# First Gram by whole 64x64 blocks, and a new order of the copies, roundings and second solver in the head of a fused attention and MLP kernel

## The chip, the cores and the metric

The kernel runs on one core of a Trainium2 chip. The metric is the time of one execution in microseconds, as the device measures it; three runs were made of the kernel before. One further execution was profiled. The engines are TensorE (PE in the profile, with its weight loads as PEld), VectorE (DVE), ScalarE (ACT), GpSimd (POOL) and SyncE (SP, which issues most DMAs).

## What is computed

Three stages follow one another. The first is a chunked delta-rule attention, the second an MLP with a gate that mixes along the sequence, the third another MLP; here they are in the reference, cut down:

```python
k_n = k / (norm(k, axis=-1) + 1e-06)            # batch 4, heads 8, seq 768, dim 48
for t in range(S):
    y[t] = q[t] @ state
    state = state + beta[t] * outer(k_n[t], v[t] - k_n[t] @ state)
x = y as (4, 768, 384)
h = gelu(x @ w_in)                               # 384 -> 1024, tanh form
u, v = h[..., :512], h[..., 512:]
gated = u * (w_sg @ layernorm(v, g_ln) + b_sg)   # w_sg mixes the 768 positions
x = x + gated @ w_out
xk, xr = mu_k * x + (1 - mu_k) * x_prev, mu_r * x + (1 - mu_r) * x_prev
out = sigmoid(xr @ w_r) * (relu(xk @ w_k) ** 2 @ w_v)
```

## The kernel before, in words

**Attention.** The 768 steps are cut into 12 chunks `s` of 64 steps, two chunks making one of NG = 6 groups `g`. The 32 pairs of batch and head lie as 16 columns on two halves of the partitions, and in two halves `o` of 8 columns each. For a group, `gram(g)` forms k k^T: for each of four blocks `i` PE makes 64 small products (32x32 and 64x32, L331 and L333) into a PSUM bank, then ACT copies the diagonal 32x32 blocks into GD and the off-diagonal ones into GL (both L340). `solver(g)` on DVE transposes GD (L358), normalizes, and inverts the unit triangular 32x32 blocks by products and sums (L353, L391); its last instruction is the transposition into DT (L438). `couple(g, k)` then multiplies GL with DT on PE (L452) and copies back on ACT (L455); a chunk's stage `st_n` needs it (`joined`).

For each chunk and half run five stages: `st_rq` (state times k and q on PE, L493 and L496; a copy r32 on ACT for group 0, L468, else an addition on DVE, L470; two copies of Q on ACT, L508, and masks on POOL, L509), `st_d` (DT times r32, L516; copy u1 on ACT, L521), `st_n` (L529, copies L535), `st_s` (the state's update, L544, copies L550) and `st_y` (L558, copy yst L563, then the stores to xT by SP). `scale_v` on POOL (L460) scales the values by the norms that solver(0) gave. A fixed list `slots` sets the order of the stages, one slot after another; `run` issues a slot, calls `tick` three times and then `fill`.

**Projections.** When both chunks of a group have their y, `x_split` makes the high part of x on ACT (L118) and the low part on POOL (L121); `push` then puts the units of that group on a list: `v_units` (PE L628, ACT L637 with the gelu, then a layernorm stream) and `u_units` (PE L680). `fill(n)` issues n products' worth of them; a v unit is ready when 6 and a u unit when 12 of the roundings of w_in are done. Where units run out, `keep_warm` issues products over a tile of zeros instead (L719), into a bank that nothing reads.

**Roundings.** The weights are split into a high and a low part that PE multiplies in three terms. One split is a job `narrow`: a DMA into `raw`, a conversion on ACT (L162), four steps on DVE (L167, L169, L171, L173), an addition on POOL (L175), the high half on ACT (L118), the low half on POOL (L121). There are three buffers `raw` and two `na`. The twelve jobs of w_in (six for the v columns, named wiv, six for the u columns, wiu) come first, then those of w_out and w_k.

**What sets the order.** PE, ACT, DVE and POOL are scheduled by hand: each engine does its instructions in the order in which the program issues them. `background(t)` gives out t units of time among three kinds of streams (ln, solve, jobs) in proportion to SHARE, with `spent` the account; an action put off by `after(n, f)` is done n points later. `point` counts the ticks. Ahead of the stages a prologue issues the first two Grams, the whole of solver(0), and what is in the list `rest`, one entry a step.

The lines that set the second solver and the first couples in order:

```python
        keep_warm(JS)
        point[0] = 0
        for e in streams:
            e[0] = 0
        later += [(3 + k, lambda k=k: couple(0, k)) for k in range(2)]
        ...
            if n == 0 and g + 1 < NG:
                streams.append([point[0] + SOLVE0, solver(g + 1), "solve"])
            background(BUDGET * (B0 if g == 0 else 1))
```

The functions that the change touches, whole:

Of the kernel before, what the change touches and what calls it, by code (L numbers as in the profile page):

```python
# [7 lines left out]
F32 = mybir.dt.float32  # L8
# [12 lines left out]
P = 128  # L21
C = 64
# [12 lines left out]
SV = 60  # L35
B0 = 1.0
PRE = 0.8
GRAM0 = 17
SOLVE0 = 1
# [9 lines left out]
LAGC = 2  # L49
JS = 18  # L50
NT_ = (3, 3, 3)
LNW = 1
LAGX = 6
LAGE = (4, 1)
LASTP = 134
FROM = 125
LAGU = 5
COST = dict(rq=1.05, d=0.8, n=0.8, s=0.85, y=1.1)
SHARE = ((1, 12, 1), (1, 4, 1), (2, 8, 2))
NRAW = 3  # L60
# [24 lines left out]
def fused_kernel(  # L85
# [142 lines left out]
    def slot(tag, shape, dtype=F32):  # L228
        return wq.tile(shape, dtype, name="s" + tag, tag=tag)
# [13 lines left out]
    with ExitStack() as at:  # L243
# [41 lines left out]
        def bank():  # L285
# [9 lines left out]
               ap1.tile([P, NU, 32], F32, name="GL")]  # L295
        DTb = [slot(W0[3], [P, NU, 32]), ap1.tile([P, NU, 32], F32, name="DT")]
        V.memset(Dm, 0.0)
        unit = ap1.tile([P, P], F32, name="unit")
# [19 lines left out]
        def gram(g, parts=((0, 64),)):  # L318
# [3 lines left out]
            def half(i, c0, c1, j):  # L322
# [13 lines left out]
                if j:  # L336
# [6 lines left out]
            return [[(0, lambda i=i, j=j, c=c: half(i, *c, j)) for j in range(2)]  # L343
                    for c in parts for i in range(4)]

        Yt = ap1.tile([P, 16, 16], F32, name="Yt")
# [9 lines left out]
        def solver(g):  # L356
# [62 lines left out]
            for last in (0, 1):  # L419
# [9 lines left out]
                for i, (ov, args) in enumerate(ops):  # L429
                    tv, t = product(*args)  # L430
                    yield t
                    if g == 0 and last and i == 1:
                        V.memset(warm, 0.0)
                    if g == 0 and last and i == 2:
                        scale_v(0)
                    yield total(ov, tv, t)
# [115 lines left out]
        def st_y(s, o):  # L552
# [13 lines left out]
            if s % 2:  # L566
                store_x(g, o, ysts[o])
                after(LAGX if g < NG - 1 else LAGE[o], lambda: splits.append((g, o)))
            if o == 1:
# [25 lines left out]
        def x_split(g, o):  # L595
# [8 lines left out]
            split(A, G if g < NG - 1 else V, xs, xh, xl)  # L604
            after(LAGU, lambda: push(g, o, xh, xl))
            return True
# [85 lines left out]
        def fill(n):  # L692
# [14 lines left out]
            if n > 0 and point[0] < 144:  # L707
                idle[0] += min(n, WARM) if point[0] <= 36 else n
                keep_warm(int(idle[0]))
                idle[0] -= int(idle[0])  # L710
# [66 lines left out]

        early(1, 0.01)
        for o in range(2):
            load_q(0, o)  # L780
        load_tok(0)
        diag = gram(0, ((0, 32), (32, 64)))
        for job in diag[:4]:
            for _, f in job:
                f()
            early(1, NPRE)
        streams.append([point[0], solver(0), "solve"])
# [3 lines left out]
        def whole(job):  # L791
            for _, f in job:
# [3 lines left out]
                 ((st_n, 0, 0), (st_rq, 1, 0)), ((st_d, 1, 0), (st_s, 0, 0), (st_y, 0, 0))]  # L796
        rest = [lambda j=j: whole(j) for j in diag[4:]]
        k = 0
        while any(e[2] == "solve" for e in streams):
            early(1, PRE)  # L800
            k += 1
            if k == 2:
# [4 lines left out]
                nc.sync.dma_start(out=mu_sb, in_=mu)  # L807
            if 0 in neTs and 1 not in GDs:
                after(SV, lambda: scale_v(1))
                body = st_rq(0, 0)  # L810
                rest.append(lambda: next(body))
                rest += [lambda j=j: whole(j) for j in gram(1)]
            if rest:
                rest.pop(0)()
        for f in rest:
            f()
        next(body, None)
        next(body, None)
        keep_warm(JS)
# [4 lines left out]
        later[:] = [(i, f) for i, (_, f) in enumerate(later)]  # L824
        later += [(3 + k, lambda k=k: couple(0, k)) for k in range(2)]
        used[0] = 0

        def tick():
# [3 lines left out]
            if nn == 0 and 0 <= gg and gg + 2 < NG:  # L832
                grams.extend(gram(gg + 2))
            if n == 0 and g + 1 < NG:
                streams.append([point[0] + SOLVE0, solver(g + 1), "solve"])
# [362 lines left out]
```

## Time and profile before

| | us |
|---|---|
| median of three runs | 776.47 (773.41 to 778.66) |
| the profiled execution | 771.39 |
| its span | 769.7 |
| PE busy | 697.1 (91%) |
| DVE busy | 507.0 (66%) |
| ACT busy | 372.9 (48%) |
| POOL busy | 200.6 (26%) |

The mean granted clock of PE in that execution is 0.968 of full. Shares of busy time are means over the three stages of the program; the head, in which the first two solvers run, is a little over an eighth of the span. The chain that ended last has 70% on PE and 12% on DVE. In a row of the timeline stand the start in us from the start of the span, the duration, the engine, the line, the operation, what it writes and reads with the names of the program's tiles, shapes, the count, and in brackets how long the engine idled before and what released it. Names are those of the storage: `sg`, `ms`, `rk`, `qk` and so on are buffers that several tiles share.

### The profile page before, as it was taken

To read this page: it belongs to the slowest core of one execution; us is meant where nothing else is said; L and a number is where in the kernel's file an instruction comes from. 1 tells how busy PE (TensorE), PEld (TensorE's weight loads), DVE (VectorE), ACT (ScalarE), POOL (GpSimd) and SP (SyncE) were. 2 spreads that over 40 slices of the span, in tenths; PEclk is the share of its full clock that TensorE was granted. 3 is DMA by queue.
4 is the path that set the end of the run, shared out by engine and by line. 5 is a ranking of instruction groups with operands and counts; after the bars stand their busy time and mean duration, and the time that the engine had idled before them with its cause. 6 is when DMAs were issued, how large, how long until landed. Compare 5 with 4: busy or idle time off the path is not lost.

```text
span 769.7 us, 24933 instructions
## 1 busy us (share of the span) xinstructions
PE 697.1 (91%) x10820; PEld 648.8 (84%) x10820; DVE 507.0 (66%) x1071; ACT 372.9 (48%) x752; POOL 200.6 (26%) x246
## 2 busy tenths in 40 slices
PE   3559799898998998888889979999999999999998
PEld 3437688787887886687889979999999999999997
DVE  6989999697797884532286867289564564563441
ACT  3236576766765767653332322147454453462330
POOL 3034635353454554430235341210000000000000
PEclk9978899999999999999989999999999999999999
DMA  8413445565565566556467562327000000000000
GB/s 238 93 41 100 131 123 153 129 185 163 148 185 155 159 171 181 194 149 198 143 229 244 178 195 79 110 87 194 22 11 32 21 11 32 21 10 32 11 22 32
DMA packets 82159, 88.76 MB, mean 115 GB/s; under 512 B 24704, under 2 KB 65024, under 8 KB 82048
## 3 DMA queue, kind: packets, MB, share of 16 engines
q1 hardware_dynamic: 76816, 77.92, 34.2%
q0 software_dynamic: 4800, 9.04, 4.3%
q8 instruction: 85, 1.39, 0.7%
q14 instruction: 26, 0.21, 0.1%
q10 hardware_dynamic: 432, 0.20, 0.1%
HBM read 56.60 MB, written 25.82 MB: 107 GB/s over the span
## 4 chain that ended last, share of the span: by engine, by line
PE 70%; DVE 12%; DMA 5%; issue 4%; POOL 3%; ACT 2%; SPq 1%; POOLq 0%; DVEq 0%; ACTq 0%
PE ms L149 36%; PE ms L944 7%; PE ms L628 6%; PE ms L680 5%; PE ms L558 3%; DVE sg L353 3%; PE rk L516 2%; PE sps L544 2%; PE rk L529 2%; PE rk L493 2%; PE ms L452 2%; POOL na L175 2%; DVE sg L391 1%; PE ms L331 1%; DVE Yt L391 1%
## 5 line engine op out<-in xcount | busy, mean ns | idle before, releaser
L149 PE MATMUL ms<-wvh,sl 128*128 128x384 f32 x192 | 64.6, 336 | 0.0
L149 PE MATMUL ms<-wvl,sh 128*128 128x384 f32 x192 | 64.5, 336 | 0.0
L149 PE MATMUL ms<-wvh,sh 128*128 128x384 f32 x192 | 64.5, 336 | 0.0
L149 PE MATMUL ms<-xm_hi,sw0h 128*128 128x384 f32 x192 | 64.2, 335 | 0.0
L149 PE MATMUL ms<-xm_hi,sw0l 128*128 128x384 f32 x192 | 64.2, 334 | 0.0
L149 PE MATMUL ms<-xm_lo,sw0h 128*128 128x384 f32 x192 | 64.2, 334 | 0.0
L175 POOL TENSOR_TENSOR na<-na,raw 128x256 int32<-128x256 int32 (+2 forms) x43 | 38.4, 894 | 98.3 <-DVE na L173 52.1
L121 DVE TENSOR_TENSOR sl<-sg,sh 128x384 fp32r<-128x384 f32 x64 | 35.7, 557 | 30.3 <-ACT sh L118 30.2
L944 PE MATMUL ms<-sw0h,g 128*128 128x384 f32 x192 | 50.3, 336 | 1.7 <-DVE g L121 1.7
L118 ACT ACTIVATE sh<-sg 128x384 fp32r<-128x384 f32 x64 | 33.5, 524 | 36.3 <-DVE sg L1118 36.3
L944 PE MATMUL ms<-ws1h,g 128*128 128x384 f32 x192 | 49.9, 334 | 0.0
L680 PE MATMUL ms<-xh,wiu_hi 128*128 128x256 f32 x144 | 40.2, 298 | 7.5 <-ACT v L637 7.5
L353 DVE TENSOR_TENSOR sg<-sg,Yt 128x512 f32<-128x512 f32 (+10 forms) x78 | 44.5, 570 | 1.6
L1134 DVE TENSOR_TENSOR sg<-sg,ms 128x384 f32<-128x384 f32 x24 | 13.3, 554 | 46.2 <-PE ms L149 46.2
L1118 DVE TENSOR_TENSOR sg<-sg 128x384 f32<-128x384 f32 x64 | 35.4, 553 | 11.5 <-ACT sg L1117 11.4
L1117 ACT ACTIVATE sg<-ms 128x384 f32<-128x384 f32 x64 | 30.8, 482 | 24.2 <-PE ms L149 24.0
L118 ACT ACTIVATE gh<-w 128x384 fp32r<-128x384 f32 x32 | 16.6, 524 | 53.1 <-DVE w L1031 53.1
L680 PE MATMUL ms<-xh,wiu_lo 128*128 128x256 f32 x144 | 39.6, 294 | 0.0
L680 PE MATMUL ms<-xl,wiu_hi 128*128 128x256 f32 x144 | 39.4, 293 | 0.0
L118 ACT ACTIVATE xm_hi<-sg 128x384 fp32r<-128x384 f32 x48 | 23.4, 517 | 31.7 <-PE ms L149 30.5
L149 PE MATMUL ms<-gh,wo_hi 128*128 128x384 f32 x96 | 34.5, 359 | 4.2 <-ACT gh L118 4.2
L509 POOL TENSOR_SCALAR_AFFINE_SELECT SQ<-SQ 64x512 f32<-64x512 f32 x36 | 27.4, 761 | 38.3 <-ACT SQ L508 32.3
(236 smaller groups left out, 2219.2 us busy)
## 6 DMA issues: line engine op xcount, KB each, us to landing
u_d<-ug SPq DMA_DIRECT2D x24, 256.0 KB, 3.5
u<-u_d SPq DMA_DIRECT2D x16, 384.0 KB, 4.8
vn_d<-v SPq DMA_DIRECT2D x22, 256.0 KB, 3.6
vk<-in_vk_dram SPq DMA_DIRECT2D x24, 192.0 KB, 4.1
vk<-in_vk_dram SPq DMA_DIRECT2D x12, 384.0 KB, 4.8
out_dram<-sg SPq DMA_DIRECT2D x24, 192.0 KB, 1.9
SQ<-in_q_d_dram SPq DMA_DIRECT2D x36, 96.0 KB, 4.3
xT<-yst SPq DMA_DIRECT2D x23, 144.0 KB, 4.1
```

What stands on the lines that cost most here:

```text
L118: A.activation(hi, src, AF.Copy)
L121: eng_lo.tensor_tensor(lo, src, hi.bitcast(F32), op=ALU.subtract)
L149: T.matmul(pt, lhsT=a, rhs=b, start=(i == 0), stop=(i == n - 1))
L175: G.tensor_tensor(a.bitcast(I32), a.bitcast(I32), w_lo.bitcast(I32), op=ALU.add)
L353: V.tensor_tensor(tv, vw(a_t, a_off, a_dims), vw(b_t, b_off, b_dims), op=ALU.mult)
L509: G.affine_select(out=pt, in_=pt, pattern=[[0, 8], [1, C]], compare_op=ALU.is_gt, fill=0.0, base=0, channel_multiplier=-1)
L558: T.matmul(yps[b0:b0 + 64, (0, 1, 2, 6, 3, 4, 5, 7)[p], :], lhsT=cur[h][:, p, 0:64], rhs=cur[h][:, p, D:], start=True, stop=True)
L628: T.matmul(vstat[g, b], lhsT=a[:, c], rhs=w[:, c], start=first, stop=last)
L680: T.matmul(vstat["u"][:, 2 * P * d:2 * P * d + 2 * P], lhsT=w[:, c, ds_], rhs=a[:, c].rearrange("p b t -> p (b t)"), start=first, stop=last)
L944: T.matmul(pt[:, :DM], lhsT=v[:, ds_], rhs=w, start=(c == 0 and i == 0), stop=(c == 5 and i == 2))
L1117: A.activation(r, pt[:, :DM], AF.Relu)
L1118: V.tensor_tensor(r, r, r, op=ALU.mult)
```

## The change

The first Gram's blocks 2 and 3 are made by a new function `gram_whole`: one 64x64 product for each column and half (16 a block instead of 64 smaller ones), and copies by quadrants of 32 partitions. The diagonal copies follow at once, on ACT for block 2 and on DVE for block 3 (whose bank is the one of `qk`); the off-diagonal ones are put on the list `rest`. Ten warming products (JS0) stand at the start of PE, and the zeros that they read are written first on DVE.

The remaining steps of the first `st_rq` go onto the list `rest`, so that their copies on ACT stand ahead of two roundings; `scale_v(0)` is issued when its norms exist, not inside the solver. JS grows from 18 to 44 products. The second solver is put on the streams directly at point 0, ahead of the others and with the accounts at zero, with a share of 8 instead of 4. The second half of the first couple comes at point 8 instead of 4. For group 0 the split of x comes 4 points after its store instead of 6, and the push 3 points after the split instead of 5 (LAG0). `fill` puts in at most 4 warming products for a slot everywhere, not only up to point 36.

```diff
-B0 = 1.0
+B0 = 1.05
+JS0 = 10
-JS = 18
+JS = 44
+LAG0 = (4, 3)
-SHARE = ((1, 12, 1), (1, 4, 1), (2, 8, 2))
+SHARE = ((1, 12, 1), (1, 8, 1), (2, 8, 2))
...
+        V.memset(warm, 0.0)
         V.memset(Dm, 0.0)
...
+        def gram_whole(i):
+
+            t, GL = kT[i // 2], GLs[0]
+            gps = bank() if i < 3 else ps2.tile([P, 8, C], F32, name="qk", bufs=1)
+            for p in range(8):
+                u = (i % 2) * 8 + p
+                for h in range(2):
+                    r = 64 * (1 - h)
+                    T.matmul(gps[r:r + 64, p, :], lhsT=t[r:r + 64, u, :],
+                             rhs=t[r:r + 64, u, :], start=True, stop=True)
+            for r in (0, 64, 32, 96):
+                c = r % 64
+                x = GD[r:r + 32, :, 8 * i:8 * i + 8].rearrange("p j u -> p u j")
+                if i == 2:
+                    A.activation(x, gps[r:r + 32, :, c:c + 32], AF.Copy, scale=-1.0)
+                else:
+                    V.tensor_scalar(x, gps[r:r + 32, :, c:c + 32], -1.0, None, op0=ALU.mult)
+
+            def off():
+                for r in (32, 96):
+                    A.activation(GL[r:r + 32, 8 * i:8 * i + 8, :], gps[r:r + 32, :, 0:32],
+                                 AF.Copy, scale=-1.0)
+
+            return off
...
-                    if g == 0 and last and i == 1:
-                        V.memset(warm, 0.0)
-                    if g == 0 and last and i == 2:
-                        scale_v(0)
...
-                after(LAGX if g < NG - 1 else LAGE[o], lambda: splits.append((g, o)))
+                after((LAGX if g else LAG0[0]) if g < NG - 1 else LAGE[o],
+                      lambda: splits.append((g, o)))
...
-            after(LAGU, lambda: push(g, o, xh, xl))
+            after(LAGU if g else LAG0[1], lambda: push(g, o, xh, xl))
...
-                idle[0] += min(n, WARM) if point[0] <= 36 else n
+                idle[0] += min(n, WARM)
...
+        keep_warm(JS0)
...
-        for job in diag[:4]:
+        for job in diag[:2]:
             for _, f in job:
                 f()
             early(1, NPRE)
+        rest = []
+        for i in range(2, 4):
+            rest.append(gram_whole(i))
+            early(1, NPRE)
...
-        rest = [lambda j=j: whole(j) for j in diag[4:]]
+        rest += [lambda j=j: whole(j) for j in diag[4:6]]
...
             if 0 in neTs and 1 not in GDs:
+                scale_v(0)
...
                 rest += [lambda j=j: whole(j) for j in gram(1)]
+                rest += [lambda: next(body, None)] * 2
...
-        next(body, None)
-        next(body, None)
         keep_warm(JS)
...
-        later += [(3 + k, lambda k=k: couple(0, k)) for k in range(2)]
+        later += [(3 + 5 * k, lambda k=k: couple(0, k)) for k in range(2)]
         used[0] = 0
+        spent[:] = [0] * 3
+        streams.insert(0, [0, solver(1), "solve"])
...
-            if n == 0 and g + 1 < NG:
+            if n == 0 and 0 < g < NG - 1:
                 streams.append([point[0] + SOLVE0, solver(g + 1), "solve"])
```

In the changed kernel the lines have other numbers: L338 to L362 lie some 3 further, the solver's lines 28 and the stages' 24 further (L358 is L386, L438 is L462, L521 is L545), and the roundings' 2 (L167 is L169, L118 is L120).

What this does to the order on DVE, between the last sum of the first solver and the beginning of the second. Before:

```order
L391 TENSOR_REDUCE sg2_109<-sg3_110 128x4x16
L438 STREAM_TRANSPOSE sw0l1_114<-sg2_109 128x32x32
L173 SCALAR_TENSOR_TENSOR na_687<-raw_278,na_687 128x256
L820 TENSOR_SCALAR m1_sb_66<-mu_sb_65 128x6
L167 TENSOR_SCALAR na_765<-raw_731 128x256
L167 TENSOR_SCALAR na_767<-raw_733 128x256
L169 TENSOR_SCALAR na_765<-na_765 128x256
L169 TENSOR_SCALAR na_767<-na_767 128x256
L171 TENSOR_SCALAR na_765<-na_765 128x256
L171 TENSOR_SCALAR na_767<-na_767 128x256
L358 STREAM_TRANSPOSE sg0_107<-sg1_108 128x1024
```

The same place now:

```order
L419 TENSOR_REDUCE sg2_109<-sg3_110 128x4x16
L462 STREAM_TRANSPOSE sw0l1_114<-sg2_109 128x32x32
L175 SCALAR_TENSOR_TENSOR na_610<-raw_277,na_610 128x256
L850 TENSOR_SCALAR m1_sb_66<-mu_sb_65 128x6
L386 STREAM_TRANSPOSE sg0_107<-sg1_108 128x1024
L169 TENSOR_SCALAR na_714<-raw_659 128x256
L390 TENSOR_SCALAR ss_716<-sg0_107 128x32
```

Six rounding steps (`na<-raw` and `na<-na`) that stood ahead of the second solver's transposition now follow it. From one transposition into DT to the next, 21 rounding steps stood between the second solver's instructions before and 12 do now; in the first solver there are 7 in both.

On ACT, where the first chunk's u1, state and y are copied and the second group is coupled (`wiu_hi` is a rounding's high half, `sw0h1` the second GL). Before:

```order
L118 ACTIVATE wiu_hi_93<-na_1169 128x256
L162 ACTIVATE raw_1182<-raw_1182 128x256
L340 ACTIVATE sg1_108<-ms_1384 128x8x32
L340 ACTIVATE GL_113<-ms_1384 128x256
L521 ACTIVATE u1_1489<-rk_1327 128x384
L550 ACTIVATE sw0h2_120<-sps0_102 48x8x48
L550 ACTIVATE sw0l2_121<-sps0_102 48x8x48
L563 ACTIVATE yst_1087<-ms_1472 128x8x64
L118 ACTIVATE wiu_hi_93<-na_1267 128x256
```

The same place now:

```order
L120 ACTIVATE wiu_hi_93<-na_1103 128x256
L164 ACTIVATE raw_1109<-raw_1109 128x256
L120 ACTIVATE wiu_hi_93<-na_1299 128x256
L545 ACTIVATE u1_1424<-rk_1254 128x384
L574 ACTIVATE sw0h2_121<-sps0_102 48x8x48
L574 ACTIVATE sw0l2_122<-sps0_102 48x8x48
L587 ACTIVATE yst_1017<-ms_1407 128x8x64
L479 ACTIVATE sw0h1_112<-ms_1437 32x512 x2
L120 ACTIVATE wiu_hi_93<-na_1346 128x256
```

Two roundings now stand ahead of u1 and the first couple copies follow y directly. Six of the twelve roundings of w_in (all of wiu) now have their additions behind the second DT; before it were two. POOL has its six additions and six low halves in that order, with the masks of one chunk between, and the low part of the first block of x behind all of them.

## Rows read from the trace of the kernel before

**Rows 1.** Busy us (instructions) by stretch: start:end, length, engines, PEclk, DMA share, GB/s.

```profile
core 0: us, PE busy (x) PEld busy (x) DVE busy (x) ACT busy (x) POOL busy (x), PEclk, DMA share, GB/s
0.00:12.04 12.04, 3.21 (x223) 3.08 (x224) 7.71 (x17) 4.07 (x7) 4.97 (x13) 1.00 0.72 194
0.00:100.00 100.00, 64.89 (x2317) 50.70 (x2317) 87.76 (x212) 43.14 (x93) 37.21 (x52) 0.88 0.44 118
...
92.60:99.30 6.70, 6.59 (x201) 5.32 (x202) 6.22 (x21) 3.20 (x7) 3.40 (x5) 0.50 0.33 86
...
143.80:147.10 3.30, 3.30 (x79) 2.96 (x79) 2.99 (x19) 2.24 (x5) 0.28 (x2) 0.50 0.35 120
```

**Rows 2.** Timeline of DVE around the first two solvers.

```profile
10.28 0.75 DVE L173 SCALAR_TENSOR_TENSOR na<-raw,na 128x256 uint32<-128x256 uint32 x2
14.54 1.25 DVE L358 STREAM_TRANSPOSE sg<-sg 128x1024 f32<-128x1024 f32 x1 [3.51 <-ACT sg L340]
...
46.51 1.92 DVE L438 STREAM_TRANSPOSE sw0l<-sg 128x1024 f32<-128x1024 f32 x1
48.30 0.39 DVE L173 SCALAR_TENSOR_TENSOR na<-raw,na 128x256 uint32<-128x256 uint32 x1
...
50.83 0.29 DVE L167 TENSOR_SCALAR na<-raw 128x256 uint32<-128x256 uint32 x1 [1.87 <-POOL wiv_lo L121]
...
52.78 1.23 DVE L358 STREAM_TRANSPOSE sg<-sg 128x1024 f32<-128x1024 f32 x1
...
90.65 1.92 DVE L438 STREAM_TRANSPOSE DT<-sg 128x1024 f32<-128x1024 f32 x1
```

**Rows 3.** Timeline of ACT: the first Gram, and behind the second DT.

```profile
9.26 0.44 ACT L162 ACTIVATE raw<-raw 128x256 int32<-128x256 uint32 x1 [0.22 <-DMA raw<-in_w_in_dram]
...
13.92 0.80 ACT L340 ACTIVATE sg<-ms 128x256 f32<-128x256 f32 x2
...
96.57 2.40 ACT L455 ACTIVATE sw0h<-ms 32x512 f32<-32x512 f32 x4
99.28 0.49 ACT L521 ACTIVATE u<-rk 128x384 f32<-128x384 f32 x1 [0.31 <-ACT sw0h L455]
```

**Rows 4.** Timeline of PE: three places where it had waited.

```profile
12.05 0.21 PE L333 MATMUL ms<-sw0l 64*32 64x32 f32 x1 [2.67 <-issue]
...
50.42 0.76 PE L516 MATMUL rk<-r,sw0l 32*32 32x48 f32 x52 [3.50 <-ACT r L468]
...
92.71 0.49 PE L452 MATMUL ms<-DT,sw0h 32*32 32x32 f32 x11 [2.96 <-DVE na L167]
```

**Rows 5.** Timeline of POOL around the second DT.

```profile
85.55 1.39 POOL L175 TENSOR_TENSOR na<-na,raw 128x256 int32<-128x256 int32 x1 [1.68 <-DVE na L173]
87.46 1.79 POOL L121 TENSOR_TENSOR wiu_lo<-na,wiu_hi 128x256 fp32r<-128x256 f32 x1 [0.53 <-ACT wiu_hi L118]
90.87 0.65 POOL L509 TENSOR_SCALAR_AFFINE_SELECT sw0h<-sw0h 64x512 f32<-64x512 f32 x1 [1.62 <-ACT sw0h L508]
...
95.37 0.73 POOL L175 TENSOR_TENSOR na<-na,raw 128x256 int32<-128x256 int32 x1
96.62 0.73 POOL L121 TENSOR_TENSOR wiu_lo<-na,wiu_hi 128x256 fp32r<-128x256 f32 x1 [0.53 <-ACT wiu_hi L118]
...
102.67 1.69 POOL L121 TENSOR_TENSOR xl<-xT,xh 128x768 fp32r<-128x768 f32 x1 [5.07 <-ACT xh L118]
```

**Rows 6.** The chain that ended last, in order of time: start us, us, what.

```profile
102.15 0.80 PE rk L529 x32
...
104.05 3.38 PE ms L628 x14
...
140.82 2.03 issue
...
284.16 1.09 PE ms L719 x5
...
331.42 0.74 POOL na L175
...
333.37 1.15 PE ms L558 x32
```

## The prediction

> **What bounds the kernel now.** I read the busy times by stretch first, then the timelines of DVE, ACT, PE and POOL over the first 105 us, then the chain that ended last. In the first 100 us PE is busy for 64.9 us and DVE for 87.8 [rows 1]; from 104 us on the chain lies almost wholly on PE [rows 6]. So in the head of the program DVE sets the pace and afterwards PE does, and a microsecond won in the head is kept only if PE gets its work earlier too.
>
> The head in DVE's rows [rows 2]: the first solver begins with the transposition at 14.54 and ends with the one that stops at 48.43 (46.51 + 1.92); the second runs from 52.78 to 92.57 (90.65 + 1.92). I call 92.57 D. PE stood still for 2.96 us until D and then began the second couple at 92.71 [rows 4]. From D it took until 104.36 (102.67 + 1.69) that POOL had the low half of the first block of x [rows 5], and the projection units, begun at 104.05 [rows 6], could go on: D + 11.8. From there PE is the bound.
>
> **The change part by part.**
>
> *First Gram and the copies.* DVE has its first roundings done at 11.03 (10.28 + 0.75) and then waits until 14.54 [rows 2], because the copies of the last Gram block, two from 13.92 on, stand on ACT behind two roundings [rows 3]. PE also had a hole: 2.67 us before 12.05, released by nothing the profile shows [rows 4]; 223 products were recorded ahead of it [rows 1]. The new order puts the four copies of block 2 on ACT ahead of the roundings and those of block 3 on DVE, and has 10 + 2 x 64 + 2 x 32 = 202 products at most up to there, so it ends before such a hole. ACT can't copy before the second raw conversion, 9.26 + 0.44 = 9.70 [rows 3]; four copies at 0.40 (two took 0.80) end at 11.3. DVE's four quadrant copies from PSUM are in no row: by DVE's step over as many elements, 0.29 [rows 2], 1.2 us together, by twice ACT's 0.40 [rows 3] 3.2; I take a little above the lower, which is DVE's own, 1.4. Transposition at 11.03 + 1.4 = 12.4: 2.1 us earlier, bounds 0.3 to 2.3. The ten warming products stand ahead of the first block, whose data PE waits for anyway, and cost nothing; if they held it up, it would be by 10 x 0.22 (five of them took 1.09 [rows 6]) = 2.2 us, and the gain here would be gone.
>
> The Trainium skill (Runtime: NRT & Kernel Launch, Instruction fetch mechanics) says that instructions come in blocks of 256 whose loading is mostly hidden. Here there is a hole of 2.67 us at 12.05 with no other releaser [rows 4], so the trace does not bear out "hidden" in this stretch. By a hidden loading the hole has another cause and need not move with the count of products: block 3 would end near 12.7 and the transposition near 14.1.
>
> *Second solver at once.* DT(0) ends at 48.43 - 2.1 = 46.3. Before, DVE then issued seven rounding steps, one of which waited 1.87 us for POOL, and started solver 1 at 52.78 [rows 2]. Now one rounding step (0.39 [rows 2]) and the small mu row stand between: start at 46.8. The first solver's 33.9 us (14.54 to 48.43) held 7 rounding steps by the order, the second's 39.8 (52.78 to 92.57) held 21: (39.8 - 33.9)/14 = 0.42 us a step with the collisions in it. The new order leaves 12: 33.9 + 5 x 0.42 = 36.0, and D falls to 82.8, 9.8 earlier. Bounds: 7 steps' worth 80.7, 21 steps' worth 86.6. PE's own chain starts earlier as well (it waited 3.50 for ACT's r32 copy until 50.42 [rows 4], and that copy now stands ahead of the roundings) and reaches the couple some 8 us before D: the 44 warming products, the couple split in two and the extra copies are all hidden there, and if they cost 5 us more it would still be nothing.
>
> *What was put off.* Six of the twelve roundings of w_in now come after D. The order on ACT shows what is queued behind them: the copies of u1, of the state, of y and of the couple, and POOL has all six differences ahead of the remainder of x. One rounding on POOL, ACT, POOL takes 1.98 us (95.37 to 96.62 + 0.73 [rows 5]). ACT's prices [rows 3]: u1 0.49; a state copy 0.5, as u1's; a couple copy 2.40/4 = 0.6, and 0.6 for y; a raw conversion 0.44; the Gram pair 0.80; the n copies 1.0 as the state's, the Q copies 1.2 as the couple's (estimates); a high half 0.4, of which the cycle holds one. In steps from D: DVE's last step 0.39; two cycles, to 4.4, the second one's ACT half done at 3.6; ACT then has 0.5 + 1.0 + 0.6 + 1.2 and the next high half 0.4, to 7.3; POOL's low half 0.73, to 8.0; DVE's steps for the next rounding, which waited for that buffer, 3 x 0.29 + 0.39 = 1.3 [rows 2], to 9.3; two cycles to 13.3, ACT free at 12.5; 0.4 + 0.8 + 1.0 + 1.2, to 15.9; a mask on POOL 0.65 [rows 5]; the sixth cycle to 18.6; the remainder of x 1.7: D + 20.3. That is 8.5 later after D than before, and 82.8 + 20.3 = 103.1 against 104.36: only 1.3 us are kept. The x stores wait on SP behind the three raw loads and land near D + 12, so they are covered.
>
> *The rest of the sum.* At that point PE before had done one n and one rq stage more, 0.80 + 1.10 (102.15 to 104.05 [rows 6]): +1.9. The order of PE has seven warming products more ahead of the point where both programs' sequences meet again, 0.22 each (1.09/5 [rows 6]): +1.5. Further on the groups of up to nine warming products are cut to four, seven fewer by the order: -1.5. PE's granted clock was 0.50 of full, the 1.2 GHz level, at 92.6 to 99.3, right behind the 2.96 us of idling [rows 1, 4]; the longest idling will lie ahead of the couple again, 20 us before the dense units, but PE waits often between. If such a stretch of 6.7 us fell on the dense units, half of it would be lost: 0 to +3.4; I take +0.5. The 2.03 us hole at 140.82 [rows 6] and the 3.3 us at 0.50 behind it [rows 1] may fall elsewhere or not at all: 0 to -3.7, I take -1.9. One rounding of w_k leaves the tail, where the chain is off PE for 1.95 us, from POOL's add at 331.42 to 333.37 [rows 6]: 0 to -2, I take -1.0. The changed shares and the later second half of the first couple are inside D.
>
> Sum: -1.3 + 1.9 + 1.5 - 1.5 + 0.5 - 1.9 - 1.0 = -1.8 us. The profiled execution took 771.39 (span 769.7), so 769.6; it lies 5.1 below the median of the runs, 776.47, and on that scale the forecast is 774.7: no change. (About 1%, 7.8 us, is what a measurement of this kernel can tell.)
>
> **The rivals.**
>
> *The lead at D is kept.* If roundings, copies and couple overlap better than my steps, so that the x point again comes 11.8 us after D, the whole 9.8 passes: -9.8 + 1.9 - 1.0 = -8.9, 767.5. For it: ACT and POOL were busy for 43 and 37 of the first 100 us [rows 1]. Against it: ACT and POOL work strictly in their written order, and u1 stands behind two roundings that DVE cannot finish before D + 1.1. Chance 0.27.
>
> *DVE and POOL block each other in the put-off roundings.* In the rows there are cycles of 1.98 us and one of 3.70 (85.55 to 89.25, an add of 1.39 and a difference of 1.79 [rows 5]). After D DVE runs almost nothing but rounding steps, and these meet POOL's. If the five cycles behind the first take 3.7, that is 5 x 1.72 = 8.6 later, and with the holes staying (+1.9) the sum is -1.8 + 10.5 = +8.7: 785.2. It is slower by over 1% from 3.5 us a cycle on. Against it: the last cycle before ran at 1.98. Chance 0.13. The Trainium skill (SBUF — State Buffer, Who interferes with whom) states how: the two engines share a pair of ports, and in some of DVE's modes, or where DVE reads two operands, one of them waits for the other's instruction. The add of 1.39 beside one of 0.73 [rows 5] agrees.
>
> *The first copies don't come early.* If block 3 is late or a quadrant copy costs 0.69, DT(0) and D come 1.7 us later: 776.4, still no change; this lies in the forecast's own case.
>
> **How the numbers follow.** No change (own range 769 to 782: D's bounds are 2.1 less and 3.8 more, the clock up to 2.9 more, the holes and the tail up to 2.8 less or 2.9 more, not all at once) 0.60; the lead kept 0.27; blocked 0.13. For 8 in 10 the range reaches into both rivals: 766.5 to 784. The chances are those of the cases: faster 0.27, within 1% 0.60, slower 0.13.
>
> **What would show it.** Right: the first solver's transposition near 12.4, the second's last one ending near 83; PE idle 5 to 10 us before the couple; after it ACT waiting for POOL's adds with u1 behind them; the x remainder done 18 to 23 us after D; PE at the 1.2 GHz level somewhere between D and 110. Wrong: a remainder of x within 14 us of D, or a solver 1 longer than 38 us, or POOL adds of 1.4 us in a row.

## The result, and the profile after

The changed kernel takes 781.4 us in the median of eleven runs (778.56 to 790.61), the kernel before 774.32 in eleven (771.40 to 780.66). The ratio is 1.0085, with a 95% interval of 1.0056 to 1.0114: slower by 0.85%, 6.6 us. The forecast of 774.7 us had said a ratio of 0.998. Runs over 1.5% above the fastest of their kernel, here the one of 790.61 us, are not in the ratios.

The profiled execution took 781.40 us with a span of 779.7 (before 771.39 and 769.7), so 10.0 us more; it lies at the median of its kernel, that of before at the lower end of its own. First the head, on DVE: start, duration, engine, line, operation, what it writes and reads, count, and the idle time before with its releaser.

```profile
10.80 0.76 DVE L175 SCALAR_TENSOR_TENSOR na<-raw,na 128x256 uint32<-128x256 uint32 x2
11.47 2.42 DVE L365 TENSOR_SCALAR sg<-qk 32x256 f32<-32x256 f32 x4
14.01 1.25 DVE L386 STREAM_TRANSPOSE sg<-sg 128x1024 f32<-128x1024 f32 x1
...
46.76 1.92 DVE L462 STREAM_TRANSPOSE sw0l<-sg 128x1024 f32<-128x1024 f32 x1
48.53 0.41 DVE L175 SCALAR_TENSOR_TENSOR na<-raw,na 128x256 uint32<-128x256 uint32 x1
48.85 0.15 DVE L850 TENSOR_SCALAR m_sb<-mu_sb 128x6 f32<-128x6 f32 x1
48.91 1.24 DVE L386 STREAM_TRANSPOSE sg<-sg 128x1024 f32<-128x1024 f32 x1
...
83.30 1.98 DVE L462 STREAM_TRANSPOSE DT<-sg 128x1024 f32<-128x1024 f32 x1
```

The first transposition starts at 14.01 against 14.54 [rows 2], the second solver at 48.91 against 52.78, and D, the end of the second DT, is at 85.28 (83.30 + 1.98) against 92.57: 7.3 us earlier. The same stretch on POOL and on PE, behind D:

```profile
85.61 0.73 POOL L177 TENSOR_TENSOR na<-na,raw 128x256 int32<-128x256 int32 x1 [0.89 <-DVE na L175]
86.88 0.73 POOL L123 TENSOR_TENSOR wiu_lo<-na,wiu_hi 128x256 fp32r<-128x256 f32 x1 [0.53 <-ACT wiu_hi L120]
...
88.82 0.86 POOL L123 TENSOR_TENSOR wiu_lo<-na,wiu_hi 128x256 fp32r<-128x256 f32 x1 [0.53 <-DMA raw<-in_w_in_dram]
...
97.77 0.87 POOL L123 TENSOR_TENSOR wiu_lo<-na,wiu_hi 128x256 fp32r<-128x256 f32 x1 [0.53 <-ACT wiu_hi L120]
...
101.98 0.77 POOL L177 TENSOR_TENSOR na<-na,raw 128x256 int32<-128x256 int32 x1
103.28 0.73 POOL L123 TENSOR_TENSOR wiu_lo<-na,wiu_hi 128x256 fp32r<-128x256 f32 x1 [0.53 <-ACT wiu_hi L120]
104.01 1.69 POOL L123 TENSOR_TENSOR xl<-xT,xh 128x768 fp32r<-128x768 f32 x1
```

```profile
103.99 0.50 PE L653 MATMUL ms<-wiv_hi,xh 128*128 128x512 f32 x1 [1.75 <-ACT xh L120]
...
105.75 0.50 PE L653 MATMUL ms<-wiv_hi,xl 128*128 128x512 f32 x1 [1.03 <-POOL xl L123]
...
142.77 0.21 PE L334 MATMUL ms<-kT 64*32 64x64 f32 x1 [2.38 <-DMA kT<-in_kt_d_dram]
...
155.26 1.50 PE L744 MATMUL ms<-warm 128*128 128x512 bf16 x3
...
161.16 1.04 PE L744 MATMUL ms<-warm 128*128 128x512 bf16 x4
162.13 0.87 PE L553 MATMUL rk<-u,GL 32*32 32x48 f32 x32
```

The low half of x is done at 105.70 (104.01 + 1.69), that is D + 20.4, against 104.36, D + 11.8, before [rows 5]: of the 7.3 us won at D nothing is left, and 1.3 more are lost. I call A the place where the two programs' sequences on PE meet again, the stage n ahead of the first units of group 1: at 162.13 here, at 151.23 before. Busy us (instructions) by stretch, with the granted clock in the third column from the end; first the kernel before, from the low half of x to A and from A on, then the changed kernel:

```profile
104.36:151.23 46.87, 43.79 (x1292) 38.40 (x1291) 40.70 (x97) 32.33 (x63) 19.08 (x27) 0.96 0.52 143
151.23:345.00 193.77, 175.82 (x4773) 152.79 (x4773) 138.17 (x293) 129.79 (x252) 92.31 (x115) 0.98 0.60 168
```

```profile
105.70:162.13 56.43, 53.43 (x1393) 45.94 (x1394) 45.06 (x119) 34.16 (x68) 20.59 (x29) 0.82 0.49 138
162.13:354.50 192.37, 175.18 (x4765) 152.82 (x4765) 138.16 (x288) 128.94 (x249) 91.11 (x113) 0.97 0.59 165
...
105.75:109.90 4.15, 4.15 (x13) 2.97 (x15) 3.78 (x20) 2.35 (x3) 0.88 (x2) 0.59 0.56 121
...
142.80:161.20 18.40, 17.99 (x491) 15.55 (x492) 11.00 (x40) 9.42 (x19) 4.01 (x9) 0.54 0.45 123
```

So the 10.0 us of this pair of executions lie at one place: +1.3 up to the low half of x, +9.6 from there to A (56.43 - 46.87), -0.9 from A to the end. PE's idle time in that stretch is the same in both (3.1 us before and 3.0 now, length less busy); it is busy 9.6 us longer. The seven warming products at 155 and 161 take 2.5 of them, and the one n and one rq stage that are done later 1.9 by their time before (0.80 + 1.10 [rows 6]). The rest, some 5, I put down to the clock: granted 0.82 against 0.96. It is low for 4 us at the first dense units (0.59) and for 18 us behind 142.8 (0.54, next to the 1.2 GHz level). This second stretch begins right behind the 2.38 us in which PE waited for a load of k.

That wait is new. SP's queue shows why; before, then after:

```profile
126.63 0.58 SPq L272 DMA_DIRECT2D vk<-in_vk_dram  x1
127.31 0.38 SPq L265 DMA_DIRECT2D kT<-in_kt_d_dram  x1
129.08 0.33 SPq L669 DMA_DIRECT2D vn_d<-v  x1
```

```profile
135.23 0.58 SPq L274 DMA_DIRECT2D vk<-in_vk_dram  x1
135.91 1.09 SPq L694 DMA_DIRECT2D vn_d<-v  x1
137.05 0.43 SPq L267 DMA_DIRECT2D kT<-in_kt_d_dram  x1
```

Units are pulled forward (LAG0), so the first layernorm store `vn_d` now stands ahead of the load of k, and the load is issued 1.1 us later for that. Before, it was issued at 127.31 and its Gram block began at 133.49, 6.2 us later, without waiting. Now PE comes to the block 3.3 us after the issue (142.77 - 2.38 - 137.05), so the store's 1.1 us are the smaller part of the wait.

### The profile page after: what moved, and what is told of

Same layout as the page of the kernel before. It is cut to its first block, busy times and chain, and to the rows that moved or that the text cites. A ratio compares the mean times of both kernels' runs of the same rounds, so it can differ in the third digit from the quotient of the medians.

```text
span 779.7 us, 24621 instructions
## 1 busy us (share of the span) xinstructions
PE 715.4 (92%) x10661; PEld 658.8 (84%) x10661; DVE 511.8 (66%) x1075; ACT 374.4 (48%) x756; POOL 199.2 (26%) x246
## 3 DMA queue, kind: packets, MB, share of 16 engines
q8 instruction: 83, 1.36, 0.7%
## 4 chain that ended last, share of the span: by engine, by line
PE 66%; DVE 12%; DMA 9%; issue 4%; ACT 4%; POOL 4%; SPq 1%; POOLq 0%; ACTq 0%; DVEq 0%
PE ms L151 36%; PE ms L976 7%; PE ms L653 5%; PE ms L705 5%; DVE sg L381 3%; PE ms L582 2%; PE rk L540 2%; PE sps L568 2%; PE rk L553 2%; PE rk L517 2%; DVE sg L419 2%; POOL na L177 1%; DMA raw<-in_w_v_dram 1%; PE ms L476 1%; PE ms L334 1%
## 5 line engine op out<-in xcount | busy, mean ns | idle before, releaser
L120 ACT ACTIVATE sh<-sg 128x384 fp32r<-128x384 f32 x64 | 33.5, 524 | 36.3 <-DVE sg L1150 36.3
L1166 DVE TENSOR_TENSOR sg<-sg,ms 128x384 f32<-128x384 f32 x24 | 13.3, 554 | 46.2 <-PE ms L151 46.2
L1150 DVE TENSOR_TENSOR sg<-sg 128x384 f32<-128x384 f32 x64 | 35.4, 553 | 11.5 <-ACT sg L1149 11.4
L120 ACT ACTIVATE gh<-w 128x384 fp32r<-128x384 f32 x32 | 16.6, 523 | 53.0 <-DVE w L1063 53.0
L151 PE MATMUL ms<-gh,wo_hi 128*128 128x384 f32 x96 | 34.7, 361 | 5.2 <-ACT gh L120 5.2
L120 ACT ACTIVATE xm_hi<-sg 128x384 fp32r<-128x384 f32 x48 | 23.4, 517 | 31.7 <-PE ms L151 30.5
```

Source lines behind the costliest of these rows:

```text
L120: A.activation(hi, src, AF.Copy)
L151: T.matmul(pt, lhsT=a, rhs=b, start=(i == 0), stop=(i == n - 1))
L1150: V.tensor_tensor(r, r, r, op=ALU.mult)
```

## The experiments

Ratios are to the kernel before, run beside each group on the same chip, with 95% intervals; its medians were 774.55 us beside e1 to e4, 777.05 beside e5 to e8, 777.74 beside e9 to e12, 777.96 beside e13 to e15 and 777.55 beside e16 to e18. Most have ten runs; e1 has six, e4 and e16 four. Where an expectation speaks of the changed kernel's 781.4 us, the ratio to compare is 1.0085.

**e1: the lags of group 0's x as before.**

```diff
-LAG0 = (4, 3)
+LAG0 = (6, 5)
```

> The changed kernel with only the split and push of group 0's x back at 6 and 5 points. Theory A (the lead at D is lost because PE then waits for x and because long stretches run at the low clock): PE does one n and one rq stage more ahead of the first units and does not idle the 2.8 us at 102.2 to 105.8; the units then begin at the full level, and units do not run out near 160: about 2.8 + 1.8 + 1.5 us less than the changed kernel, 775 to 777, and the first unit still not before 105. Theory B (the remainder of x alone sets the time): the remainder is done at the same place, 105.7, and the time stays at 780 to 782.

Measured: 1.0081 (1.0053 to 1.0110). The low half of x was done only at 109.41, since the split now stands behind further work on ACT and POOL; A was at 161.89 with no warming product ahead of it and no wait for k. Neither theory: the x point moved by 3.7 us, and A and the time stayed. It also shows the loss of 0.8% without the wait for k.

**e2: the second solver started as before.**

```diff
-SHARE = ((1, 12, 1), (1, 8, 1), (2, 8, 2))
+SHARE = ((1, 12, 1), (1, 4, 1), (2, 8, 2))
...
-        spent[:] = [0] * 3
-        streams.insert(0, [0, solver(1), "solve"])
...
-            if n == 0 and 0 < g < NG - 1:
+            if n == 0 and g + 1 < NG:
```

> The changed kernel with the second solver started as before (behind the roundings, share 4, accounts not reset). Theory A: D goes back to about 91 but fewer roundings stand behind it; the remainder of x comes about 12 to 14 us after D, at 103 to 105; the time moves by less than 3 us, 778 to 783. Theory B: with two roundings behind D instead of six the x point is earlier, and the time goes down to 775 to 777.

Measured: 1.0081 (1.0045 to 1.0117). D went to 93.75, 8.5 us later, and the low half of x came at 105.28, D + 11.5. Theory A: the lead at D is worth nothing, because the roundings behind it take just as long.

**e3: 18 warming products ahead of the chain.**

```diff
-JS = 44
+JS = 18
```

> The changed kernel with 18 instead of 44 warming products ahead of the chain; PE waits 5.3 us behind them anyway, so no stage begins later or earlier by this alone. Theory A, in the form that the place of the unexplained holes in PE's instruction stream decides the long stretch at half clock: 26 products fewer move every later hole, the hole of 2.38 us at 140.4 goes elsewhere and the stretch at half clock behind it changes by several us: 775 to 779 or, if it falls worse, over 783. Rival (the stretch follows the order of the stages, not the holes): 780 to 782, and the stretch from 143 to 161 is at half clock again.

Measured: 1.0014 (0.9976 to 1.0051): by the mean nearly the whole loss is gone, by an edit of 26 products in a stretch in which PE waits. The profiled execution had the wait for k (2.30 us) and half the clock behind it all the same, and A at 161.28; at 779.26 us it was the third longest of the ten, so it does not show where the 5.5 us of the median went. Theory A's second form had the size right, and its mechanism, the moving of this one wait, wrong.

**e4: no cap on warming.**

```diff
-                idle[0] += min(n, WARM)
+                idle[0] += min(n, WARM) if point[0] <= 36 else n
```

> The changed kernel without the new cap: up to 9 instead of 4 warming products where units run out. By my step in the prediction they only cost: 12 products more, 0.22 us each at the full level, 2.6 us more, 783 to 785. Rival (the cap lets the clock fall): the stretches at half clock near 160 and 290 to 345 get shorter and the time goes down to 777 to 780.

Measured: 1.0101 (1.0062 to 1.0139), 1.2 us over the changed kernel, within the noise; A was 1.65 us later at 163.78, with five more warming products ahead of it. No gain from more warming products where units run out is shown, so the rival falls; that they cost, as the step had it, is not clear of the noise.

**e5: 26 short products instead of the 26 long ones.** Behind `keep_warm(JS)`, with JS = 18:

```diff
+        o = bank()[:].rearrange("p a b -> p (a b)")
+        for _ in range(26):
+            T.matmul(o[:, 0:32], lhsT=warm, rhs=warm[:, 0:32], start=True, stop=True)
```

> The changed kernel with 18 warming products and 26 products of 32 columns in place of the other 26 of 512 columns: PE's instruction stream has the same count as in the changed kernel, but 6 us less activity before the chain. If the place of the instructions decides (holes): 779 to 783, as the changed kernel's 781.4, not 776 as with 18 alone. If the long burst of activity itself costs clock later: 774 to 778, as with 18 alone.

Measured: 1.0074 (1.0044 to 1.0104), as the changed kernel. The 26 took 0.80 us, and PE then waited 10.4. So the loss goes with the count of products, not with the length of the burst.

**e6: 44 products in the kernel before.**

```diff
-JS = 18
+JS = 44
```

> The kernel before with 44 instead of 18 warming products; the 26 more take some 6 us of the 3.5 us in which PE waits for ACT plus the stretch behind. If the burst itself costs clock: 779 to 782, 5 us over the kernel before. If the place of the instructions decides: any value within 5 us of 774, and no reason for just this sign. By my step in the prediction (hidden, and nothing if they cost 5 us more, since PE then waits for DVE): 774 to 776.

Measured: 0.9961 (0.9929 to 0.9994). The same edit that costs 0.7% in the one kernel gains 0.4% in the other.

**e7: the first part alone.** The kernel before with `gram_whole`, JS0, the early zeros, and the new list `rest`; JS, LAG0 as (6, 5), the cap, SHARE, B0, the couples and the second solver as before.

> The kernel before with the first part alone: blocks 2 and 3 whole, copies by quadrant, ten warming products at the start, first copies ahead of the roundings; 18 products ahead of the chain, solver 1, LAGs, shares, couples and cap as before. DVE's first transposition near 14.0 as in the changed kernel (14.54 before), D about 0.5 to 1 us earlier: 773 to 775 by the path; with holes elsewhere up to 4 us to either side.

Measured: 0.9967 (0.9927 to 1.0006, eight runs), no difference shown. The first transposition came at 13.38, D at 93.28, later than before by 0.7: the lead of 1.2 us was mostly lost inside the first solver, which ran to 48.15 against 48.43.

**e8: the split of x one rounding earlier.**

```diff
-JS = 44
+JS = 18
-LAG0 = (4, 3)
+LAG0 = (3, 4)
```

> The changed kernel with 18 products and the split of group 0's x after 3 points instead of 4, which puts it ahead of the last rounding of w_in on ACT and POOL. If the rounding in front of it sets the x point: remainder of x at 102 to 104 instead of 105.7, and 2 us less than with 18 products alone (775.9): 773 to 775. If the store of y or the masks set it: no change, 775 to 777.

Measured: 0.9969 (0.9935 to 1.0004), and the low half of x done at 103.62, D + 18.4, where e3 had it at D + 20.4: the sixth rounding had held it up for some 2 us. A gain in time over e3 is not shown; the intervals overlap. POOL's order in that execution:

```profile
101.06 0.74 POOL L533 TENSOR_SCALAR_AFFINE_SELECT sw0l<-sw0l 64x512 f32<-64x512 f32 x1
101.90 1.72 POOL L123 TENSOR_TENSOR xl<-xT,xh 128x768 fp32r<-128x768 f32 x1
103.58 0.74 POOL L177 TENSOR_TENSOR na<-na,raw 128x256 int32<-128x256 int32 x1
```

**e9: the loads of k on ACT's queue** (changed kernel), **e10**: the same on the kernel before, **e11**: on e8, **e12**: on e8 with 44 products.

```diff
-        def load_k(s):
+        def load_k(s, q=nc.sync):
...
-            nc.sync.dma_start(out=kT[s], in_=kt_d[s])
+            q.dma_start(out=kT[s], in_=kt_d[s])
...
-                load_k(s + NKT)
+                load_k(s + NKT, nc.scalar)
```

> The changed kernel with the loads of k for chunks 4 to 11 issued on ACT's queue, right behind the stage that frees the buffer, instead of on SP's behind stores of the layernorm. Theory C (units pulled forward put a vn_d store ahead of the k load on SP; PE then waits 2.38 us at 140.4 and runs at half clock until 161): the wait is gone, the stretch from 143 to 161 is mostly at full clock, A (the first units of group 1) is 5 to 8 us earlier, 774 to 777. Rival (the clock falls there whatever comes before): the wait goes but the half clock stays, 778 to 780.

> The kernel before with the same move of the k loads. There the load lands some 0.6 us ahead of its first use and PE does not wait for it, so by theory C nothing changes: 773 to 778 beside 774 to 777. If it is faster by over 3 us, the k loads cost something in both kernels and e9 tells less.

> e8 (18 products, split of group 0's x after 3 points) with the move of the k loads. There the wait for k was 1.03 us and a half-clock stretch followed it: theory C gives 1 to 5 us less than e8, 769 to 774, that is a ratio of 0.990 to 0.996 to the kernel before. Rival: as e8, 0.997.

> The same with 44 products. If the place of PE's instructions decides the 5 us between 44 and 18 products (e5 against e3), it is 3 to 6 us over e11 or under it. If that difference came through the wait for k and the stretch behind it, it is within 2 us of e11.

Measured: e9 1.0046 (1.0022 to 1.0071), e10 1.0010 (0.9972 to 1.0048), e11 0.9963 (0.9935 to 0.9992), e12 1.0047 (1.0016 to 1.0078). In e9 the wait for k is gone, and the same stretches read:

```profile
142.80:161.20 18.40, 15.71 (x502) 12.62 (x494) 10.05 (x43) 13.02 (x26) 5.57 (x9) 0.91 0.64 158
...
105.97:157.12 51.15, 46.48 (x1393) 40.21 (x1393) 43.60 (x123) 34.10 (x68) 20.03 (x30) 0.97 0.56 151
```

The clock is at 0.91 and 0.97 instead of 0.54 and 0.82, and A is at 157.12, 5.0 us earlier, as theory C said. But from A to the last product that execution took 619.9 us against 613.9: what was won at A was not there at the end. Over the runs the move is worth 0.4% by the means with 44 products (1.0085 to 1.0046, and the intervals overlap), and nothing with 18 (e8 to e11) or in the kernel before.

That the wait brings the low clock is not shown either. In e9 PE stood still for 2.12 us in the same Gram, with no releaser, and the clock stayed. The profiled execution of e5 has the wait for k ahead of the same products, and its clock in the 18.4 us behind it is 0.82, not 0.54:

```profile
142.06 0.24 PE L336 MATMUL ms<-kT 64*32 64x64 f32 x1 [2.12 <-issue]
```

```profile
143.43 0.28 PE L334 MATMUL ms<-kT 64*32 64x64 f32 x1 [2.34 <-DMA kT<-in_kt_d_dram]
...
143.40:161.80 18.40, 16.48 (x573) 13.76 (x574) 11.48 (x40) 12.49 (x24) 4.72 (x8) 0.82 0.52 137
```

Nor is the wait the loss of the change: e1 loses 0.8% without it, and e12 against e11 is again 0.8% for 26 products, while PE waits for k in neither.

**e13 to e15: the place of the edges.** In every trace PE has holes that nothing releases, and they stand at the same counts of products. Busy (and count) from the start up to two such holes and the rows behind the holes, first of the kernel before, then of the changed kernel:

```profile
0.00:185.10 185.10, 145.25 (x4686) 120.37 (x4687) 162.48 (x378) 101.72 (x207) 75.89 (x100) 0.93 0.50 135
0.00:189.40 189.40, 148.66 (x4814) 123.36 (x4815) 164.22 (x379) 104.36 (x212) 76.44 (x100) 0.93 0.50 136
...
185.64 0.21 PE L333 MATMUL ms<-sw0l 64*32 64x64 f32 x1 [1.15 <-issue]
...
189.92 0.20 PE L493 MATMUL rk<-sw0l,kT 64*64 64x48 f32 x1 [0.87 <-issue]
```

```profile
0.00:193.10 193.10, 160.16 (x4434) 126.78 (x4434) 165.00 (x379) 101.88 (x208) 76.79 (x101) 0.83 0.48 130
0.00:200.70 200.70, 166.38 (x4689) 132.28 (x4689) 169.50 (x387) 106.78 (x218) 77.39 (x102) 0.84 0.48 131
...
193.40 0.24 PE L568 MATMUL sps<-SQ,vk 64*48 64x48 f32 x1 [0.52 <-issue]
...
201.17 0.25 PE L517 MATMUL rk<-sw0h,kT 64*64 64x48 f32 x1 [0.85 <-issue]
```

And of the run with 64 short products (e14), where the hole behind 4689 products falls on other stages again:

```profile
0.00:196.90 196.90, 157.83 (x4689) 128.03 (x4689) 168.68 (x387) 106.85 (x218) 76.12 (x102) 0.85 0.49 132
0.00:200.50 200.50, 160.16 (x4816) 130.18 (x4816) 170.67 (x390) 108.85 (x222) 77.43 (x104) 0.85 0.48 131
...
197.46 0.27 PE L520 MATMUL qk<-sw0h,kT 64*64 64x64 f32 x1 [1.16 <-issue]
...
201.52 1.00 PE L476 MATMUL ms<-DT,sg 32*32 32x32 f32 x30 [1.74 <-issue]
```

4434 to 4689 is two times 127.5, 4686 to 4814 is 128, 4689 to 4816 is 127: the holes lie a multiple of 128 recorded products apart (a record is missing now and then), in all three programs at the same counts. With a weight load each, 128 products are 256 instructions. What differs is the stage on which they fall.

The traces also show what PE waits for there. The DMA queue q8, which the profile calls "instruction", moves one packet of 16 KB for about 128 products: 83 for the 10661 products of the changed kernel (1.36 MB).

```profile
PE 715.4 (92%) x10661; PEld 658.8 (84%) x10661; DVE 511.8 (66%) x1075; ACT 374.4 (48%) x756; POOL 199.2 (26%) x246
...
q8 instruction: 83, 1.36, 0.7%
```

Ahead of the holes that end at 193.40 and 201.17 such a packet lands at 191.84 and 199.79. In all twenty traces every hole without a releaser ahead of 345 us (over 0.15 us, 377 of them) stands at such an edge and ends 1.1 to 1.9 us behind the landing of a packet. So the holes are waits for the next block of instructions.

The edits are e5's loop with 128 and with 64 products, and with 26 on the kernel before:

> The changed kernel with 18 warming products and 128 products of 32 columns behind them, which lie in the 10 us in which PE waits for ACT. In the traces the holes that nothing releases stand at the same counts of products in every kernel, a multiple of 128 apart (223, 478, 605; 4306, 4434, 4561, 4689, 4816). Theory D (those holes are blocks of PE's instructions, and which stage a block's edge falls on decides the 5 to 7 us between 44 and 18 products): with 128 more every later edge falls where it fell with 18 alone, so 774 to 778, not 781 to 784 as with 26 more. Rival (more products or more instructions ahead of the chain cost, whatever their place): 781 to 786.

> The same with 64 products of 32 columns: by theory D a third place of the edges, anything from 772 to 784, another value than the rival's, which is 781 to 785 (between e5's 26 and e13's 128).

> The kernel before with 26 products of 32 columns behind its 18: by theory D the same edges as with 44 products (e6, 0.996 of before), so 0.993 to 1.000; by the rival (more instructions cost) 1.005 to 1.010.

Measured: e13 0.9988 (0.9952 to 1.0025), e14 1.0061 (1.0028 to 1.0094), e15 0.9974 (0.9943 to 1.0005). With 26, 64 and 128 short products the ratio goes 1.0074, 1.0061, 0.9988; with none it is 1.0014. The number of instructions is out as a cause, and that the loss goes at just a whole block more is what theory D said. This rests on e13: e14 would fit the rival too, and e15's interval includes 1.

**e16 to e18: where it acts.** 18 products ahead of the chain, and 26 short ones only at a later place, for e16:

```diff
+                if (s, i) == (4, 0):
+                    tiny(26)
```

(`tiny` is e5's loop.) For e17 the place is (8, 0), for e18 behind `run((st_y, 11, 1))`.

> The changed kernel with 18 warming products (the place that gave ratios of 1.0014 and 0.9988), and 26 products of 32 columns, 0.8 us, inserted on PE ahead of the first stages of chunk 4, near 150 us: ahead of that the edges of the instruction blocks lie as with 18, behind it as with 44. If the cost of the place arises ahead of 150 us: 0.999 to 1.003 of before. If behind: 1.006 to 1.010.

> The same with the 26 products ahead of the first stages of chunk 8, near 250 us. Cost ahead of 250: 0.999 to 1.003; behind: 1.006 to 1.010; spread evenly over the program: between e16 and e18.

> The same with the 26 products behind the last stage of the attention, near 345 us. The long products that follow need an edge only every 20 us, so by theory D nothing changes but the 0.8 us: 0.999 to 1.003. If it is 1.006 or more, the place acts in the two MLP stages.

Measured: e16 1.0110 (1.0014 to 1.0205, four runs only), e17 1.0048 (1.0010 to 1.0086), e18 1.0014 (0.9977 to 1.0051). Shifted from 345 us on, the edges cost nothing that these runs show; from 250 on about half, from 150 on all, though the edges ahead of that lie as in e3. So it acts in the attention's second part and seems spread over it. The intervals are wide, and that no more than half lies behind 250 rests on means that differ by less than their intervals.

Most pairs of profiled executions do not differ as the medians do, such as e3 and e5 (779.26 and 780.04 us) or e13 and e14 (781.95 and 779.70). In e11 and e12 they do (775.34 and 783.16 us; medians 774.08 and 781.52). From the low half of x to the last y these two did the same 6126 products, e11 first:

```profile
103.20:340.89 237.69, 215.61 (x6126) 186.45 (x6126) 184.09 (x411) 162.67 (x317) 109.93 (x143) 0.97 0.58 163
```

```profile
103.01:348.58 245.57, 218.89 (x6126) 188.83 (x6126) 184.17 (x411) 162.95 (x317) 110.78 (x142) 0.96 0.57 157
```

All of the difference, 7.9 us, lies here. PE idles 4.6 us longer, 3.3 of it in the holes (17.7 us against 14.4), and is busy 3.3 us longer. The low clock does not carry the loss over the runs: the mean granted clock is 0.951 in both e11 and e12, and between 0.945 and 0.948 in e3 and e13, which don't lose, and in e5 and e14, which do.

**The best versions.** e11 at 0.9963 and e6 at 0.9961 are the only two of the eighteen whose intervals stay below 1, by 0.4%: e11 is the change with 18 products, the split after 3 points and k's loads on ACT's queue; e6 is the kernel before with nothing but 26 more products at another place. That e11 owes anything to its own edits and not to the place of its edges is therefore not shown.

## Why the prediction was right or wrong

*First Gram and the copies.* Forecast 12.4 for the first transposition, measured 14.01. The four quadrant copies take 2.42 us on DVE, 0.6 each against the 0.35 that I took (1.4 in all), and ACT's 2.46 for four, not 0.40 each: a copy of 32 partitions was no cheaper than one of 128. The bounds, 1.2 to 3.2, held it; the value was taken at the wrong end. That is 1.0 us; the other 0.6 come from the first roundings, which DVE ended at 11.56 instead of 11.03. The hole stands behind 223 products as before, 2.60 us long, and so past the 202.

*Second solver at once.* The first solver took 34.7 us (forecast 33.9), the second 36.4 (36.0), D 85.28 (82.8): 2.5 late, 1.6 of it from the first transposition.

*What was put off.* The low half of x at D + 20.4, forecast D + 20.3, and the absolute place 105.70 against 103.1, late by D's 2.5. This step was right in its parts too: the second rounding behind D ended on POOL at D + 4.4 (forecast 4.4), the fifth at D + 13.4 (13.3), the sixth at D + 18.7 (18.6). So is its verdict: e2 takes the lead at D back and changes nothing. The rival that the lead is kept fell with it, and so did the one of blocking: POOL's additions behind D took 0.73 to 0.79.

*The rest of the sum.* The n and rq stages and the seven warming products were there. The clock's term was taken at 0.5 of 0 to 3.4, for a stretch at the dense units; it was about 5 in the profiled execution: some 1.7 of that at the dense units (4.15 us at 0.59), the rest over small stages behind a wait for k that I had not reckoned with. I had followed SP's queue for the stores of x, not for the loads that come behind layernorm stores when units are pulled forward. The hole of 2.03 us at 140.82 (-1.9) did go, but the wait for k, 2.38 us, took its place, and PE's idle time up to A was the same. From A on the forecast had -2.5 (warming and tail); the profiled execution has -0.9.

*The step that failed* is the sentence that the 44 warming products "are all hidden there, and if they cost 5 us more it would still be nothing". They are hidden where they stand, and they cost 0.7% elsewhere: they move every later edge of PE's instruction blocks to another stage (e3, e5, e13, e14), a cost for which the sum had no term. Without that the parts of the change do come to no change, 1.0014 (e3) and 0.9988 (e13) against the forecast's 0.998. That bears out the total and not its terms, and is in part luck. The mean granted clock of the runs was 0.957 to 0.961 for the kernel before and 0.945 and 0.9475 in e3 and e13. Against that, the profile of before has 31.6 us of block holes ahead of 345 us and those of e3 and e13 17.9 and 21.9. The sum had +0.5 for the clock and one hole, of 1.9, for all this. The same move gains 0.4% in the kernel before (e6); with short products the gain is not clear of the noise (e15).

I had seen such a hole at 12.05 and had even counted products up to it, but for one place only. The Trainium skill (Runtime: NRT & Kernel Launch, Instruction fetch mechanics) says that blocks hold 256 instructions and that crossing an edge is mostly hidden. The runs agree with the 256. On the second they agree only by count: the changed kernel's trace has 64 such packets ahead of 345 us and 17 holes. Behind 100 us, between short products, the holes are up to 3 us long, and up to 6.5 us in the head of the kernel before; moving the edges by 26 or 64 products is worth 0.6 to 0.8% of the changed kernel.

What stays open: in the profiled executions neither A, nor the time from A on, nor the sum of the holes (19.8 us in the changed kernel, 31.6 before) orders the kernels as their medians do; a single profile varies by as much as the effect. So that the place of the edges makes the loss is shown by e13 beside e3, e5 and e14; which edges cost the most, and how much of the loss is the holes themselves, is not. The mean clocks above speak against the low clock behind them.

## What to carry to other kernels

A lead on one engine is worth what the work put off behind it leaves of it: sum the queue behind the new end before counting the lead. Where a program streams thousands of short products, inserting or removing some anywhere moves all later holes, so an edit of under 1% is to be compared at several places of the edges (some short products in a gap shift them for nothing) before its parts are judged. And where units are pulled forward, look at what their stores overtake on the DMA queue.

## What was not expected of the hardware

The holes on PE that nothing releases stand at fixed counts of instructions, 128 products with their weight loads apart, whatever the program, and end 1.1 to 1.9 us behind the landing of a packet on the queue q8. 26 products of 0.03 us each, in a gap of 10 us, moved the time by 0.6% up in one kernel (e5 against e3), and by 0.3% down in the other by the mean, where the interval includes 1 (e15). A wait of 2.38 us was followed by 18 us at a granted clock of 0.54 in one program, while before a hole of 2.03 us was followed by 3.3 us at 0.50 [rows 1, 6]; what followed differed (Gram and rq products, against couple products and projection units). But in e5 the same wait, 2.34 us, ahead of the same products was followed by 0.82 over 18.4 us, so the wait and the products alone do not set it. A copy of a quadrant, 32x256 elements, took 0.6 us on DVE and on ACT, where ACT had taken 0.80 for two of 128x256 [rows 3].
